# First two token groups of an FNet and ReGLU layer: one written order on all engines, GpSimd's subtractions behind VectorE's

## The chip, the cores and the metric

One core of a Trainium2 chip runs the whole program. The metric is the device time of one execution in microseconds (us), from the median of several runs; lower is better. The kernel before took 1047.72 us (median of three runs: 1047.72, 1048.57 and 1043.9).

## The reference

For 2048 tokens x of width 640, with xn = layernorm(x) over the width:

```python
a = einsum("bsd,ed->bse", xn, dft_hid_re)
b = einsum("bsd,ed->bse", xn, dft_hid_im)
y = einsum("ts,bse->bte", dft_seq_re, a) - einsum("ts,bse->bte", dft_seq_im, b)
gate, up = xn @ W_gate, xn @ W_up
h = gate * (gate > 0) * up
return x + y + h @ W_down
```

All of it is float32. The four DFT matrices are ordinary inputs.

## The kernel before

Every product is made of three TensorE passes. An operand is split into a rounded high part and a low part (operand minus high part), and a product is high x high, then high weights x low moving data, then low weights x high moving data (`mm3`, lines 125 to 131; the passes are lines 129, 130, 131). TensorE is so the engine with the most work, and the other engines make the high and low parts. Usually ScalarE writes the high part (line 123) and VectorE subtracts it (line 124).

The first stage multiplies the layer norm of the tokens by the sequence DFT. Tokens come in eight groups (`NG`) of 128 x 2; j = 0, 1 counts the two rows of tokens that a partition holds (`SG`). A unit of work is `first_stream(c, name, g)`: one block of 128 x 1024 of the DFT (`raw`, split into `cb`) for column chunk c and group n, multiplied with the normalised tokens of that group (`xs_early` for groups 0 to 3, `xs_late` for 4 to 7). Each unit has four steps: load, prepare, run, finish. `drive(4, 2)` issues them with the loads four units ahead and the preparing two units ahead. For an engine the order of its instructions is fixed when the program is built: a scheduler orders them, except where `tc.keep_in_program_order` pins an instruction to the place in which it was written, and where `tc.issue_after` puts it behind another. SP's queue issues the loads in its own order, and each load waits there for its buffer; GpSimd's queue issues the stores and small copies.

The normalisation of a group: VectorE takes statistics (`ln_stats`, lines 203 and 204), ScalarE and VectorE make the mean's negative and the inverse root (`ln_root`, lines 210 to 217, mostly instructions on 128 x 1 or 128 x 2 elements), then the normalised high part is written by ScalarE and the low part by VectorE.

The start is special, since nothing is there yet to multiply:

- TensorE first runs 48 products on zeros (line 111).
- `first_group` (lines 283 to 320) normalises group 0 one j at a time, columns d0 (128) before d14 (256), and splits the two DFT blocks c = 0 and c = 1 of group 0 in halves of 512 columns: ScalarE the high part (line 290), GpSimd the low part (line 291). VectorE writes the tokens' low parts in line 230. A dummy on GpSimd (line 299) makes it wait for line 217 before its first subtraction.
- `first_products(j, b)` (lines 474 to 484) runs 18 products for each j. A pass is v = 0 (high x high), 1 (low tokens) or 2 (low DFT). They may be interleaved by the scheduler.
- `second_group` (lines 263 to 282) normalises group 1 whole (both j at once): ScalarE writes the high parts (line 275), VectorE the scaled tokens (278) and the low parts (280). The DFT block of that group for c = 0 is split by the ordinary `split` (lines 123 and 124), placed by the scheduler.
- `second_products(b)` (lines 446 to 455) multiplies it: for j = 0 the passes v = 0 and 2, the same for j = 1, then v = 1 for both.
- From group 2 on `layernorm(g)` (lines 236 to 261) and `product` do the same with fewer rules.

A group's tokens lie in one of four places of a shared buffer (`ln_place`), so the load of group g + 4 waits until group g's last reader is done; for group 0 that is line 258, for ScalarE.

## Time and profile before

| | |
|---|---|
| median of three runs | 1047.72 us (1043.9 to 1048.57) |
| profiled execution, first to last instruction (span) | 1043.3 us |
| lowest of the three runs, beside that span | 1043.9 us, 0.6 us above it |
| TensorE busy | 1028.4 us of the span |
| first product of the first stage | starts at 6.62 us |
| first product of the second group | starts at 18.45 us |
| mean granted TensorE clock | 0.997 |

The profile has one execution. Its own run time is not listed apart from the three; the span is the nearest to the lowest run. A row of the timeline reads: start, duration, engine, line, operation, output and inputs, shape, count, and in brackets the idle time before it with what ended it. PE is TensorE's matmul, PEld its weight load, DVE VectorE, ACT ScalarE, POOL GpSimd, SPq the queue of SyncE. Rows of consecutive instructions of a kind are merged (x2, x32), and instructions of one engine overlap by some 0.1 us in such rows. The granted clock (PEclk) is the share of full speed that the throttle let through.

### The profile page before, as it was taken

The numbers are of one execution on the slowest core, as the hardware profiler recorded it, in microseconds if no ns is written. First come the engines' busy times: TensorE is split into PE (matmuls) and PEld (weight loads), VectorE is DVE, ScalarE is ACT, GpSimd is POOL, SyncE is SP. The second block draws the span as 40 slices with busy tenths as digits, with TensorE's granted clock in tenths as the row PEclk, the third lists the DMA queues.
The fourth block names the chain that finished last, engine by engine and source line by source line (L and its number), as shares of the span: only waits on it lengthen the run. The fifth ranks groups of instructions, "written<-read, shape, count | busy, mean of one in ns | idle before, by whom it ended". The sixth has DMA issues, their size and how long they took to land.

```text
span 1043.3 us, 12416 instructions
## 1 busy us (share of the span) xinstructions
PE 1028.4 (99%) x4528; PEld 847.3 (81%) x4528; DVE 802.1 (77%) x1071; ACT 433.5 (42%) x543; POOL 95.7 (9%) x156
## 2 busy tenths in 40 slices
PE   8999999999999899899999999999999999999998
PEld 7888888888887788688888888888888888888886
DVE  7857886978979887577887988887488667786764
ACT  6654453333333443333334534343355423552521
POOL 2000010101211001421110000100000000000000
PEclk9999999999999999999999999999999999999999
DMA  7985754958867863863364566565498637986454
GB/s 294 340 247 170 261 161 140 311 205 269 305 199 259 339 203 116 251 222 143 131 206 177 203 224 232 215 237 188 145 393 287 207 111 218 366 300 233 157 159 121
DMA packets 100156, 233.29 MB, mean 224 GB/s; under 512 B 11392, under 2 KB 50816, under 8 KB 98688
## 3 DMA queue, kind: packets, MB, share of 16 engines
q1 hardware_dynamic: 83664, 166.96, 47.6%
q0 software_dynamic: 16432, 65.55, 17.4%
q8 instruction: 35, 0.57, 0.2%
q14 instruction: 25, 0.20, 0.1%
HBM read 177.41 MB, written 54.02 MB: 222 GB/s over the span
## 4 chain that ended last, share of the span: by engine, by line
PE 84%; DMA 5%; DVE 5%; issue 4%; ACT 2%; POOL 0%; SPq 0%; ACTq 0%; POOLq 0%; DVEq 0%
PE ps L131 27%; PE ps L130 27%; PE ps L129 27%; DMA z<-in_wgu 2%; DVE cb L124 1%; DMA r<-in_x 1%; DMA st<-set 1%; PE ps L1147 1%; PE ps L483 1%; ACT cb L123 1%; DMA set<-st 1%; DMA rw<-hd 1%; DVE raw L595 0%; DVE gw L770 0%; ACT gw L120 0%
## 5 line engine op out<-in xcount | busy, mean ns | idle before, releaser
L131 PE MATMUL ps<-cb,wt 128*128 128x512 f32 x390 | 151.9, 390 | 0.1
L129 PE MATMUL ps<-cb,wt 128*128 128x512 f32 x390 | 151.8, 389 | 0.0
L130 PE MATMUL ps<-cb,wt 128*128 128x512 f32 x390 | 151.7, 389 | 0.0
L124 DVE TENSOR_TENSOR cb<-rw,cb 128x1024 fp32r<-128x1024 f32 x83 | 94.2, 1135 | 66.6 <-ACT cb L123 65.9
L123 ACT ACTIVATE cb<-rw 128x1024 fp32r<-128x1024 f32 x83 | 81.9, 987 | 145.2 <-PE ps L131 125.0
L123 ACT ACTIVATE cb<-raw 128x1024 fp32r<-128x1024 f32 x78 | 82.5, 1059 | 124.9 <-PE ps L131 108.3
L124 DVE TENSOR_TENSOR cb<-raw,cb 128x1024 fp32r<-128x1024 f32 x78 | 95.1, 1221 | 41.2 <-ACT cb L123 38.0
L130 PE MATMUL ps<-xs_early,gw 128*128 128x512 f32 x260 | 101.2, 389 | 0.0
L129 PE MATMUL ps<-xs_early,gw 128*128 128x512 f32 x260 | 101.2, 389 | 0.0
L131 PE MATMUL ps<-xs_early,gw 128*128 128x512 f32 x260 | 101.1, 389 | 0.0
L130 PE MATMUL ps<-cb,xs_late 128*128 128x512 f32 x256 | 99.8, 390 | 0.9 <-DVE cb L124 0.8
L131 PE MATMUL ps<-cb,xs_late 128*128 128x512 f32 x256 | 99.7, 389 | 0.3 <-DVE xs_late L251 0.3
L129 PE MATMUL ps<-cb,xs_late 128*128 128x512 f32 x256 | 99.6, 390 | 0.4 <-ACT cb L123 0.4
L130 PE MATMUL ps<-cb,xs_early 128*128 128x512 f32 x238 | 92.8, 390 | 1.5 <-DVE cb L124 1.5
L129 PE MATMUL ps<-cb,xs_early 128*128 128x512 f32 x238 | 92.6, 391 | 1.1 <-ACT cb L123 1.1
L120 ACT ACTIVATE gw<-z 128x1024 fp32r<-128x1024 f32 (+1 forms) x52 | 57.8, 1111 | 84.2 <-DVE z L760 68.7
L131 PE MATMUL ps<-cb,xs_early 128*128 128x512 f32 x238 | 92.1, 389 | 0.0
L131 PEld LDWEIGHTS ps<-cb,wt 128*128 128x128 f32 x390 | 73.2, 188 | 15.7 <-DVE wt L124 0.5
L130 PEld LDWEIGHTS ps<-cb,wt 128*128 128x128 f32 x390 | 73.2, 188 | 15.4
L129 PEld LDWEIGHTS ps<-cb,wt 128*128 128x128 f32 x390 | 73.2, 188 | 15.2
L120 ACT ACTIVATE u<-ps 128x512 f32<-128x512 f32 x52 | 31.2, 599 | 93.0 <-PE ps L131 93.0
L770 DVE TENSOR_TENSOR gw<-z,gw 128x1024 fp32r<-128x1024 f32 (+1 forms) x52 | 64.8, 1286 | 2.3 <-ACT gw L120 2.2
(192 smaller groups left out, 1932.1 us busy)
## 6 DMA issues: line engine op xcount, KB each, us to landing
raw<-in_dft SPq DMA_DIRECT2D x94, 512.0 KB, 5.7
wt<-wparts SPq DMA_DIRECT2D x66, 256.0 KB, 3.2
z<-in_wgu SPq DMA_DIRECT2D x26, 640.0 KB, 4.0
hd<-ob POOLq DMA_DIRECT2D x26, 512.0 KB, 3.5
rw<-hd SPq DMA_DIRECT2D x24, 512.0 KB, 6.1
wparts<-pw POOLq DMA_DIRECT2D x11, 1024.0 KB, 4.1
tk<-in_dft SPq DMA_DIRECT2D x16, 512.0 KB, 6.2
rw<-pq SPq DMA_DIRECT2D x16, 512.0 KB, 7.7
```

What stands on the lines that cost most here:

```text
L120: return nc.scalar.activation(o, i, AF.Copy)
L123: nc.scalar.activation(hi, src, AF.Copy)
L124: return nc.vector.tensor_tensor(lo, src, hi.bitcast(F32), op=OP.subtract)
L129: nc.tensor.matmul(ps, wh, mh, start=first, stop=False, skip_group_check=more)
L130: nc.tensor.matmul(ps, wh, ml, start=False, stop=False, skip_group_check=more)
L131: nc.tensor.matmul(ps, wl, mh, start=False, stop=last, skip_group_check=more)
L483: nc.tensor.matmul(E[c, key], xn_part(j, d)[v == 1], b[c][0][:, int(v == 2), j], start=j == 0 and v == 0, stop=False)
L770: tt(self.w[:, 1, cs], self.z[:, cs], self.w[:, 0, cs].bitcast(F32), op=OP.subtract)
L1147: nc.tensor.matmul(B[key], wr[:, v, es], hr[:, cs], start=False, stop=v == 1, skip_group_check=not new)
```

## The change

Only the start of the first stage is rewritten.

- Loads: the order becomes tokens j = 0, DFT (c = 0, j = 0), tokens j = 1, DFT (1, 0), (0, 1), (1, 1).
- `first_group` is one loop over j. For j = 1 the normalised high parts come from ScalarE in one step out of the raw tokens (new line 315, with the bias made in line 313), VectorE centres all 640 columns behind them (line 222) and then writes the low parts (317).
- GpSimd's two subtractions of a j (new line 295) stand behind a dummy (new `behind_vector`, line 268) that reads the last column of the tokens' low parts of that j: it waits until VectorE has written them.
- `first_products` takes the passes in the order v = 0 and 1 for c = 0, v = 0 and 1 for c = 1, then v = 2 for both, and all are pinned.
- `second_group` also splits the DFT block of group 1: its high part on ScalarE (line 277) ahead of `ln_root`, its low part on VectorE (line 285) as the last instruction of the group. Everything in it is pinned.
- `second_products` are pinned (line 462), and the products of n = 1, c = 1 stand behind their last one.

The numbers of instructions stay as they were but for a second dummy on GpSimd, two more rows on VectorE and one less on ScalarE. From about 60 us on, the order of every engine's instructions is the same as before.

```diff
--- before.py
+++ after.py
@@ -260,62 +260,69 @@
         if g == NG - 1:
             nc.sync.dma_start(rows.rearrange("m (g p j) -> p m g j", p=P, j=SG), stat)
 
-    def second_group():
+    def pin(steps):
+        return [tc.keep_in_program_order(i) for i in steps]
+
+    def behind_vector(src, o):
+
+        pin([nc.gpsimd.tensor_tensor(o, src, src, op=OP.mult)])
+
+    def second_group(b, raw):
 
         xs, bs, mv = ln_tiles(1)
         js = slice(0, SG)
         nm, r = (stat[:, i, 1, js] for i in range(2))
-        with tc.issue_after(late["ln"]):
-            for i in ln_stats(1, xs, bs, mv, js):
-                pass
-            for i in ln_root(1, mv, js):
-                tc.keep_in_program_order(i)
-            nmr = mv[:, js, 6]
-            late["ln"] = tc.keep_in_program_order(nc.vector.tensor_tensor(nmr, nm, r, op=OP.mult)).ins
-            highs = [nc.scalar.activation(xn_block(1, K14, 0)[:, j], xs[:, j, K14], AF.Identity,
-                                          bias=mv[:, j, 6:7], scale=stat[:, 1, 1, j : j + 1]) for j in range(SG)]
-            for j in range(SG):
-                nc.vector.tensor_scalar(xs[:, j], xs[:, j], mv[:, j, 0:1], stat[:, 1, 1, j : j + 1],
-                                        op0=OP.subtract, op1=OP.mult)
-            low = nc.vector.tensor_tensor(xn_block(1, K14, 1), xs[:, :, K14], xn_block(1, K14, 0).bitcast(F32), op=OP.subtract)
-            keep_a21(1)
-        late["first"] = [i.ins for i in highs + [low]]
+        nmr = mv[:, js, 6]
+        pin(ln_stats(1, xs, bs, mv, js))
+        pin([nc.scalar.activation(flat(b, 0), raw, AF.Copy)])
+        pin(ln_root(1, mv, js))
+        pin([nc.vector.tensor_tensor(nmr, nm, r, op=OP.mult)])
+        pin(nc.scalar.activation(xn_block(1, K14, 0)[:, j], xs[:, j, K14], AF.Identity,
+                                 bias=mv[:, j, 6:7], scale=stat[:, 1, 1, j : j + 1]) for j in range(SG))
+        pin(nc.vector.tensor_scalar(xs[:, j], xs[:, j], mv[:, j, 0:1], stat[:, 1, 1, j : j + 1],
+                                    op0=OP.subtract, op1=OP.mult) for j in range(SG))
+        pin([nc.vector.tensor_tensor(xn_block(1, K14, 1), xs[:, :, K14], xn_block(1, K14, 0).bitcast(F32), op=OP.subtract)])
+        late["ln"] = pin([nc.vector.tensor_tensor(flat(b, 1), raw, flat(b, 0).bitcast(F32), op=OP.subtract)])[0].ins
+        late["second"] = late["ln"]
+        keep_a21(1)
 
     def first_group(b):
 
 
-        pin = lambda steps: [tc.keep_in_program_order(i) for i in steps]
         xs, bs, mv = ln_tiles(0)
         part = lambda c, j: b[c][1][:, j * CH : (j + 1) * CH]
-        high = lambda c, j: [nc.scalar.activation(b[c][0][:, 0, j], part(c, j), AF.Copy)]
-        low = lambda c, j: [nc.gpsimd.tensor_tensor(b[c][0][:, 1, j], part(c, j), b[c][0][:, 0, j].bitcast(F32),
-                                                    op=OP.subtract)]
-        j0, j1 = slice(0, 1), slice(1, 2)
+        high = lambda c, j: pin([nc.scalar.activation(b[c][0][:, 0, j], part(c, j), AF.Copy)])
+        low = lambda c, j: pin([nc.gpsimd.tensor_tensor(b[c][0][:, 1, j], part(c, j), b[c][0][:, 0, j].bitcast(F32),
+                                                        op=OP.subtract)])
         d0, d14, rest, every = slice(0, P), slice(P, 3 * P), slice(P, D), slice(0, D)
-        pin(ln_stats(0, xs, bs, mv, j0))
-        pin(ln_center(0, xs, mv, 0, d0, nc.vector))
-        pin(ln_root(0, mv, j0))
-
-        pin([nc.gpsimd.tensor_tensor(mv[:, 0, 6:7], stat[:, 1, 0, 0:1], stat[:, 1, 0, 0:1], op=OP.mult)])
-        pin(high(0, 0))
-        pin(low(0, 0))
-        h0, h14 = ln_scale(0, xs, 0, d0), ln_scale(0, xs, 0, d14)
-        pin([next(h0)])
-        pin(ln_center(0, xs, mv, 0, rest, nc.vector))
-        pin([next(h14)])
-        pin(high(1, 0))
-        pin(low(1, 0))
-        pin(h0)
-        pin(h14)
-        pin(high(0, 1))
-        pin(low(0, 1))
-        pin(ln_stats(0, xs, bs, mv, j1))
-        pin(ln_root(0, mv, j1))
-        pin(ln_center(0, xs, mv, 1, every, nc.scalar))
-        pin(ln_scale(0, xs, 1, d0))
-        pin(ln_scale(0, xs, 1, d14))
-        pin(high(1, 1))
-        late["ln"] = pin(low(1, 1))[-1].ins
+        for j in range(SG):
+            js = slice(j, j + 1)
+            places = [tokens(0)[:, j * XS + o : j * XS + o + D] for o in (0, D)]
+            pin(ln_stats(0, xs, bs, mv, js))
+            if j == 0:
+                pin(ln_center(0, xs, mv, 0, d0, nc.vector))
+            pin(ln_root(0, mv, js))
+            high(0, j)
+            nmr = mv[:, j, 6:7]
+            if j == 0:
+                h0, h14 = ln_scale(0, xs, j, d0), ln_scale(0, xs, j, d14)
+                pin([next(h0)])
+                pin(ln_center(0, xs, mv, 0, rest, nc.vector))
+                pin([next(h14)])
+            else:
+                pin([nc.vector.tensor_tensor(nmr, stat[:, 0, 0, js], stat[:, 1, 0, js], op=OP.mult)])
+                for cs in (d0, d14):
+                    pin([nc.scalar.activation(places[0][:, cs], xs[:, j, cs], AF.Identity, bias=nmr, scale=stat[:, 1, 0, js])])
+                pin(ln_center(0, xs, mv, j, every, nc.vector))
+                h0, h14 = (pin([nc.vector.scalar_tensor_tensor(places[1][:, cs], xs[:, j, cs], stat[:, 1, 0, js],
+                                                               places[0][:, cs].bitcast(F32), op0=OP.mult, op1=OP.subtract)])
+                           for cs in (d0, d14))
+            high(1, j)
+            pin(h0 if j == 0 else ())
+            pin(h14 if j == 0 else ())
+            behind_vector(places[1][:, 3 * P - 1 : 3 * P].bitcast(F32), mv[:, j, 6:7] if j == 0 else bs[:, 0, 0, 0:1])
+            low(0, j)
+            low(1, j)
 
     def token_sets(q, step, stage=stage, unit=None):
 
@@ -452,7 +459,8 @@
             for j in js:
                 for v in vs:
                     for d, key in zip((0, 1, 4), keys):
-                        nc.tensor.matmul(E[0, key], xn_part(SG + j, d)[v == 1], b[:, int(v == 2), j], start=False, stop=False)
+                        start["pe"] = pin([nc.tensor.matmul(E[0, key], xn_part(SG + j, d)[v == 1], b[:, int(v == 2), j],
+                                                            start=False, stop=False)])[0].ins
 
     def product(g, b, w, accs, first, more, extra=None):
 
@@ -474,14 +482,13 @@
     def first_products(j, b):
 
         keys = [("e1", 0), ("e1", 1), "v1"]
-        for v, cs in (((0, (0,)), (1, (0,)), (2, (0,)), (0, (1,)), (1, (1,)), (2, (1,))),
-                      ((0, (0,)), (2, (0,)), (0, (1,)), (1, (0,)), (2, (1,)), (1, (1,))))[j]:
+        for v, cs in ((0, (0,)), (1, (0,)), (0, (1,)), (1, (1,)), (2, (0, 1))):
             for c in cs:
                 for d, key in zip((0, 1, 4), keys):
                     if j == 0 and v == 0:
                         E[c, key] = bank()
-                    nc.tensor.matmul(E[c, key], xn_part(j, d)[v == 1], b[c][0][:, int(v == 2), j],
-                                     start=j == 0 and v == 0, stop=False)
+                    pin([nc.tensor.matmul(E[c, key], xn_part(j, d)[v == 1], b[c][0][:, int(v == 2), j],
+                                          start=j == 0 and v == 0, stop=False)])
 
     def resident(g, d):
         return lambda j, i: xn_part(g * SG + j, d + i)
@@ -514,31 +521,36 @@
         def load():
             if n == 0 and c == 0:
                 st = start["raw"] = [raw(), raw()]
-                for j in range(SG):
-                    ln_load(0, slice(j, j + 1))
-                    for k in range(2):
-                        i = (k + j) % 2
-                        nc.sync.dma_start(st[i][:, j * CH : (j + 1) * CH], dft[i, 0, 0][:, j * CH : (j + 1) * CH])
+                get = lambda c, j: nc.sync.dma_start(st[c][:, j * CH : (j + 1) * CH], dft[c, 0, 0][:, j * CH : (j + 1) * CH])
+                ln_load(0, slice(0, 1))
+                get(0, 0)
+                ln_load(0, slice(1, 2))
+                for i in ((1, 0), (0, 1), (1, 1)):
+                    get(*i)
                 return
             if norm is not None:
                 tc.keep_in_program_order(ln_load(norm, slice(0, SG)))
             if n > 0 or c > 1:
                 t["s"] = raw()
                 nc.sync.dma_start(t["s"], dft[c, 0, n])
+                start[c, n] = t
 
         def prepare():
             if norm == 0:
                 start["b"] = [(parts(), st) for st in start["raw"]]
                 first_group(start["b"])
                 return
-            if norm is not None:
-                (second_group if norm == 1 else lambda: layernorm(norm))()
-            if n > 0 or c > 1:
+            if norm == 1:
+                t1 = start[0, 1]
+                t1["b"] = parts()
+                second_group(t1["b"], t1["s"])
+            elif norm is not None:
+                layernorm(norm)
+            if (n > 0 or c > 1) and "b" not in t:
                 t["b"] = b = parts()
-
                 with ExitStack() as order:
-                    for i in late["first"] if (c, n) == (1, 1) else ():
-                        order.enter_context(tc.issue_after(i))
+                    if (c, n) == (1, 1):
+                        order.enter_context(tc.issue_after(late["second"]))
                     split(flat(b, 0), flat(b, 1), t["s"])
 
         def run():
@@ -549,7 +561,10 @@
                 second_products(t["b"])
                 return
             accs = [(c, ("e1", i)) for i in range(2)]
-            product(g, t["b"], resident(n, 0), accs, half == 0, half == 1, ((c, "v1"), half, half == 0))
+            with ExitStack() as order:
+                if n == 1 and c < 2:
+                    order.enter_context(tc.issue_after(start["pe"]))
+                product(g, t["b"], resident(n, 0), accs, half == 0, half == 1, ((c, "v1"), half, half == 0))
 
         def finish():
             if g == NH - 1:
```

## The prediction

> **What bounds the kernel.** The page first.
>
> ```profile
> span 1043.3 us, 12416 instructions
> ...
> PE 1028.4 (99%) x4528; PEld 847.3 (81%) x4528; DVE 802.1 (77%) x1071; ACT 433.5 (42%) x543; POOL 95.7 (9%) x156
> ```
>
> TensorE is busy for all but 14.9 us of the span, so a change of the start is worth only what it takes from or adds to TensorE's waits there. Next, TensorE in the timeline of the start, and the windows:
>
> ```profile
> 6.62 0.50 PE L483 MATMUL ps<-cb,xs_early 128*128 128x512 f32 x1 [0.30 <-ACT xs_early L229]
> 8.02 0.98 PE L483 MATMUL ps<-cb,xs_early 128*128 128x512 f32 x3 [0.89 <-DVE xs_early L230]
> 9.44 9.17 PE L483 MATMUL ps<-cb,xs_early 128*128 128x512 f32 x32 [0.44 <-DVE xs_early L230]
> 18.45 2.88 PE L455 MATMUL ps<-cb,xs_early 128*128 128x512 f32 x12
> ...
> 22.52 0.39 PE L455 MATMUL ps<-cb,xs_early 128*128 128x512 f32 x1
> 22.75 0.39 PE L130 MATMUL ps<-cb,xs_early 128*128 128x512 f32 x1
> ...
> 43.84 0.50 PE L131 MATMUL ps<-cb,xs_late 128*128 128x512 f32 x1 [0.30 <-DVE xs_late L251]
> ...
> 6.57:9.98 3.41, 2.02 (x6) 1.00 0.99 385
> 9.98:13.40 3.42, 3.42 (x9) 0.50 1.02 420
> ```
>
> Products at full clock start 0.227 us apart (22.52 to 22.75). The 36 first products need 8.2 us and take 11.8 (6.62 to 18.45). The 3.6 us over are two waits for VectorE's low tokens (line 230) and a stretch of 3.42 us at half clock (the 0.50 in the second window row; its columns are length, busy time, clock, DMA share, GB/s), in which 9 products lie where 15 would start. From 18.45 on TensorE doesn't wait, until a wait for group 4's low tokens at 43.84. All that the start could give is these 3.6 us and some 0.5 at 43.84.
>
> **The change, part by part.**
>
> ```profile
> 5.98 0.16 DVE L217 SCALAR_TENSOR_TENSOR stat<-mv 128x1 f32<-128x1 f32 x1
> 6.17 0.91 ACT L229 ACTIVATE xs_early<-r,stat 128x128 fp32r<-128x128 f32 x2
> 6.22 0.36 POOL L299 TENSOR_TENSOR mv<-stat 128x1 f32<-128x1 f32 x1 [5.77 <-DVE stat L217]
> 6.55 2.55 POOL L291 TENSOR_TENSOR cb<-raw,cb 128x512 fp32r<-128x512 f32 x2
> 6.61 2.77 DVE L230 SCALAR_TENSOR_TENSOR xs_early<-r,stat,xs_early 128x128 fp32r<-128x128 f32 x2
> 9.30 0.87 DVE L203 BATCH_NORM_STATS2 bs<-r 128x6 f32<-128x320 f32 x2
> 9.79 1.28 POOL L291 TENSOR_TENSOR cb<-raw,cb 128x512 fp32r<-128x512 f32 x1 [0.69 <-ACT cb L290]
> 10.21 0.21 DVE L204 BATCH_NORM_AGGREGATE mv<-bs 128x2 f32<-128x12 f32 x1
> 11.06 0.16 DVE L215 SCALAR_TENSOR_TENSOR mv<-mv 128x1 f32<-128x1 f32 x1
> 11.26 0.16 DVE L216 TENSOR_TENSOR mv<-mv 128x1 f32<-128x1 f32 x1
> 11.45 0.16 DVE L217 SCALAR_TENSOR_TENSOR stat<-mv 128x1 f32<-128x1 f32 x1
> 11.92 0.80 ACT L229 ACTIVATE xs_early<-r,stat 128x128 fp32r<-128x128 f32 x2
> 12.36 0.35 DVE L230 SCALAR_TENSOR_TENSOR xs_early<-r,stat,xs_early 128x128 fp32r<-128x128 f32 x1 [0.35 <-ACT xs_early L229]
> 13.03 0.47 DVE L230 SCALAR_TENSOR_TENSOR xs_early<-r,stat,xs_early 128x256 fp32r<-128x256 f32 x1
> 13.42 0.20 DVE L204 BATCH_NORM_AGGREGATE mv<-bs 128x2 f32<-128x12 f32 x1
> 14.41 0.21 DVE L204 BATCH_NORM_AGGREGATE mv<-bs 128x2 f32<-128x12 f32 x1
> 14.54 1.22 DVE L124 TENSOR_TENSOR cb<-raw,cb 128x1024 fp32r<-128x1024 f32 x1
> 16.60 0.17 DVE L274 TENSOR_TENSOR mv<-stat 128x2 f32<-128x2 f32 x1
> 16.80 1.31 ACT L275 ACTIVATE xs_early<-r,mv,stat 128x384 fp32r<-128x384 f32 x2 [1.57 <-DVE mv L274]
> 19.38 0.94 DVE L280 TENSOR_TENSOR xs_early<-r,xs_early 128x768 fp32r<-128x768 f32 x1
> 20.36 1.17 DVE L124 TENSOR_TENSOR cb<-raw,cb 128x1024 fp32r<-128x1024 f32 x1
> 23.77 0.61 DVE L246 TENSOR_SCALAR r<-r,mv,stat 128x640 f32<-128x640 f32 x1
> ```
>
> 1. *Low tokens of j = 0.* The pair of line 230 takes 0.35 and 0.47 alone (12.36, 13.03), but 2.77 beside GpSimd's two subtractions (2.55): each waits until one has ended. Behind the dummy they are alone: the second starts when ScalarE's high part is there (6.17 + 0.91 = 7.08, so 7.11) and ends at 7.58 instead of 9.38, 1.80 us sooner.
>
> 2. *GpSimd* starts its dummy 0.08 behind VectorE, as before (6.22 after 5.98 + 0.16) at 7.67, the subtractions 0.33 after it at 7.99, and they end at 9.26 and 10.54, where they ended at 7.8 and 9.1. The new pass order asks for them last: 12 products come first, 6.62 to 9.7. The first is in time, the second about 0.1 late.
>
> 3. *Statistics and root of j = 1* took 2.31 (9.30 to 11.45 + 0.16) and now start at 7.50. They fall beside the subtractions. In the trace nothing shows an instruction of one element with two inputs beside a running subtraction: line 215 starts at 11.06, at which the third (9.79 + 1.28) ends. So bounds: nothing, as the one-input lines 203 and 204 kept their time there (0.87 for two, 0.21), or a wait to the end of the second subtraction. Line 216 would be due at 7.50 + (11.26 - 9.30) = 9.46 and wait to 10.54, 1.08 us; if line 215 at 9.26 waits already, 1.28. The nearest row is line 230, the same operation with two inputs, which waited out each subtraction: I take 1.1. The root ends at 7.50 + 2.31 + 1.1 = 10.9.
>
> 4. *The rest of j = 1.* The bias (new line 313) is one step more, some 0.25 behind line 217 (an estimate: the root's own steps are 0.20 apart, 11.26 to 11.45, and this one waits for ScalarE too), and ScalarE follows 0.20 behind it (16.60 to 16.80): 11.2. Two high parts 0.80: 12.0. Then VectorE, which waits for them, centres 640 columns (0.61, as line 246) and writes the low parts (0.82 less 0.1 of overlap): 13.4, where they ended at 13.50. The early start is spent; without the wait of step 3 it is 12.3. GpSimd's second pair then runs from 13.84 to 16.4.
>
> 5. *First products.* Without the waits of 1.4 and 0.8 us the window from 6.57 has 14 starts instead of 6, so the half clock after it goes. They run into j = 1's parts instead: high tokens at 11.6 and 12.05, low ones at 13.0 and 13.4, GpSimd's at 15.1 and 16.4. The last three start from 16.45, and all end at about 17.1 instead of 18.45.
>
> 6. *Second group: what is late next.* VectorE's order is now four statistics, root, bias, scaling, low tokens, and **last** the low part of the DFT block (new line 285). In the trace that subtraction ran at 14.54, before the root, and was done at 15.76, and TensorE came at 18.45. Now: statistics from 13.3; the first aggregate 0.91 later (9.30 to 10.21), the second 0.99 after it, as 13.42 to 14.41, so at 15.2. Line 215 follows 0.85 later (10.21 to 11.06) at 16.05, which again meets GpSimd's last subtraction (to 16.4, 0.3 us); line 217 at 16.8, the bias at 17.05, the high parts from 17.25 to 18.56. Each scaling waits for ScalarE's high part of its j, and the second ends at 19.2. Then 0.94 for the low tokens and 1.2 for line 285 give **21.25** (without the waits of steps 3 and 6: 19.95).
>
> The passes of j = 0 are v = 0, then v = 2, which reads line 285's output. TensorE does three products when the first high part comes (17.96) and stands from 18.7 to 21.3. The other 15 and the product behind them need 15 x 0.227 + 0.1 = 3.5, so line 130 starts at 24.8 instead of 22.75: **2.05 us later**. Behind line 285 on VectorE stand group 2's statistics and the low part of the next block. The trace began that subtraction at 20.36; now it follows four statistics and an aggregate (1.7 by lines 203 and 204) and begins at 22.85, 2.5 us later and just in time for TensorE.
>
> 7. *What is carried to 43.84.* TensorE's 2.05 could use up the 0.46 us that it waited there, but group 4's low tokens come by VectorE, whose delay is 2.5.
>
> ```profile
> 25.66 0.89 ACT L258 ACTIVATE st<-r,stat 128x256 f32<-128x256 f32 x2
> 26.58 0.33 SPq L198 DMA_DIRECT2D r<-in_x  x1
> ...
> r<-in_x SPq DMA_DIRECT2D x1, 640.0 KB, 4.3
> ...
> 33.90 1.28 DVE L203 BATCH_NORM_STATS2 bs<-r 128x6 f32<-128x320 f32 x3 [0.94 <-DMA r<-in_x]
> 42.29 1.49 DVE L251 TENSOR_TENSOR xs_late<-r,xs_late 128x1280 fp32r<-128x1280 f32 x1
> ```
>
> Group 4's tokens are loaded by SP at 26.58, when line 258 has ended, and land 7.3 us later, at 33.9, after a wait of 0.94 on VectorE. The load of group 5's, issued just ahead of it (the row of 640 KB), took 4.3. In the new order of SP one DFT load stands ahead of it, and line 258 is some 2.85 us later (2.5 and a longer root), so the issue is at 29.4. After 4.3 us it would be there at 33.7, after 7.3 at 36.7. Group 4's statistics now also stand ahead of group 3's low tokens (0.95 us). From landing to the end at 43.78 the trace took 9.9; now it is 10.8. So the delay at 43.84 lies between 0.7 and 3.7; I take the middle, 2.2, near to TensorE's own 2.05. Later orders are unchanged.
>
> The moved loads cost nothing: they are as many bytes, and the tokens of j = 1, now third, land before 7.50.
>
> **Sum: +2.2 us**, 1043.3 to 1045.5 on the span. The lowest run, 1043.9, is 0.6 above that span, the median 1047.72 is 4.4 above it; on the median the forecast is **1049.9**. A measurement can tell about 0.5% (5.2 us) from no change, so this is "same".
>
> [...]
>
> **The rivals.**
>
> *No lock for one element.* Line 285 ends at 19.95, line 130 starts at 23.5, 0.7 late; with VectorE's 1.3 us of delay the end is +1.0: 1048.7. For: lines 203 and 204 weren't held. Against: line 230 was.
>
> *A new half clock.* If the window from 16.81 again has few products (5 or 6 starts by step 6; 6 starts before), the next runs at half. From 21.3 to 23.64 TensorE starts 5.5 products instead of 10.3, 1.1 us: +3.1, 1050.8. For: 2.02 of 3.41 us busy was followed by 0.50. Against: where the windows lie need not repeat from run to run. [...]
>
> *The gain stays (faster).* If the second group's parts were there when TensorE gets to them, the first products end at 16.15 (step 3 without wait) and 2.3 us are kept: 1045.4. For: all waits at 8.02 and 9.44 go. Against: it decides by line 285 being done before 17, and the order puts it behind two scalings that need ScalarE.
>
> *Slower by more than 0.5%.* Group 4's tokens. If their load lands 7.3 us after its issue, at 36.7, group 3's low tokens behind them are late for TensorE and group 4's end at 47.5: +3.7; with a half clock behind that stand (1.7, half of 3.42) +5.4: 1053.1. It decides from a landing at about 35. For: the 7.3 and the load now ahead of it. Against: the load of group 5 took 4.3.
>
> **How the numbers follow.** Forecast 0.40, no lock 0.22, half clock 0.20, slower 0.10, gain stays 0.08. The range reaches from the kept gain to just over the half clock with the upper end of step 7: 1045.0 to 1052.5; it leaves out the slowest. Over 0.5% faster 0.04 (half of the last rival, as the runs spread over 4.7 us), slower 0.10, within 0.86.
>
> **What would show it.** Line 230's pair in 1.0 us: step 1. Line 215 or 216 with a hole in front that ends with a subtraction: step 3; no hole: the first rival. TensorE idle before the fourth of line 462 with VectorE's line 285 as releaser: step 6. Line 130 behind line 462 at 24.8; the clock from 20.2 on; the wait before group 4's statistics: the others. The forecast is wrong if line 285 ends before 18, or if the delay is used up by later waits of TensorE.

## The result and the profile after

The kernel after takes 1051.2 us (median of 20 executions, 1046.31 to 1054.21), the kernel before 1047.16 (20 executions, 1043.9 to 1051.28): ratio 1.0036, 95% interval 1.0022 to 1.0049. So it is some 4 us slower, within the 0.5% that the forecast called "same". It stood at 1049.9, with a range of 1045.0 to 1052.5. The profiled execution of after took 1047.28 us with a span of 1045.4. That is **2.1 us** over the span of before, where the forecast had 2.2, but only half of what the medians differ by. In every run that lists both, the time is 1.7 to 2.1 us over the span. So the profiled execution of before took about 1045.1 us (an estimate from its span of 1043.3), some 2 us below its median, while that of after lies 3.9 us below its own: the two profiles are not of typical executions, and that of before isn't of the lowest run, 1043.9. Where the other half is, is the question of the experiments.

The page of after, its first lines:

```profile
span 1045.4 us, 12416 instructions
...
PE 1028.8 (98%) x4528; PEld 846.1 (81%) x4528; DVE 802.0 (77%) x1073; ACT 433.2 (41%) x542; POOL 95.5 (9%) x157
```

TensorE works as long as before (1028.8 us against 1028.4); what was added is waiting. Its timeline at the start, of after (start, length, instruction, in brackets the idle time ahead of it and what ended that):

```profile
6.65 4.77 PE L490 MATMUL ps<-cb,xs_early 128*128 128x512 f32 x18 [0.48 <-ACT xs_early L229]
11.65 1.23 PE L490 MATMUL ps<-cb,xs_early 128*128 128x512 f32 x3 [0.23 <-ACT xs_early L315]
13.12 4.14 PE L490 MATMUL ps<-cb,xs_early 128*128 128x512 f32 x15 [0.24 <-DVE xs_early L317]
17.76 0.97 PE L462 MATMUL ps<-cb,xs_early 128*128 128x512 f32 x3 [0.50 <-ACT xs_early L280]
21.14 3.74 PE L462 MATMUL ps<-cb,xs_early 128*128 128x512 f32 x15 [2.40 <-DVE cb L285]
```

The first products end at 17.26 instead of 18.61 (9.44 + 9.17 in the profile of before; its next product started at 18.45), without the old waits and without half clock. Then three products of the second group run, and TensorE stands 2.40 us for line 285, the low part of the DFT block. VectorE and GpSimd in the same view of after, where this comes from:

```profile
6.63 0.35 DVE L230 SCALAR_TENSOR_TENSOR xs_early<-r,stat,xs_early 128x128 fp32r<-128x128 f32 x1
7.13 0.48 DVE L230 SCALAR_TENSOR_TENSOR xs_early<-r,stat,xs_early 128x256 fp32r<-128x256 f32 x1 [0.15 <-ACT xs_early L229]
7.70 0.19 POOL L268 TENSOR_TENSOR mv<-xs_early 128x1 f32<-128x1 f32 x1 [7.25 <-DVE xs_early L230]
7.86 2.54 POOL L295 TENSOR_TENSOR cb<-raw,cb 128x512 fp32r<-128x512 f32 x2
9.30 1.12 DVE L215 SCALAR_TENSOR_TENSOR mv<-mv 128x1 f32<-128x1 f32 x1
10.45 0.16 DVE L216 TENSOR_TENSOR mv<-mv 128x1 f32<-128x1 f32 x1
...
12.71 0.75 DVE L317 SCALAR_TENSOR_TENSOR xs_early<-r,stat,xs_early 128x128 fp32r<-128x128 f32 x2
...
16.80 0.16 DVE L279 TENSOR_TENSOR mv<-stat 128x2 f32<-128x2 f32 x1
17.74 1.21 DVE L282 TENSOR_SCALAR r<-r,mv,stat 128x640 f32<-128x640 f32 x2 [0.78 <-ACT xs_early L280]
18.99 0.96 DVE L284 TENSOR_TENSOR xs_early<-r,xs_early 128x768 fp32r<-128x768 f32 x1
19.86 1.22 DVE L285 TENSOR_TENSOR cb<-raw,cb 128x1024 fp32r<-128x1024 f32 x1
```

Read it from the top: the low tokens are alone and short (0.35, 0.48). GpSimd then runs from 7.86 to 10.40, and line 215, one element with two inputs, takes 1.12 us instead of 0.16 and ends at 10.42, just behind GpSimd. Everything on VectorE up to line 285, the last of its written order, is late by that and by the order itself, and 285 ends at 21.08.

**A table by place.** All kernels run the same 4480 products (products of zeros not counted), so one can ask when the n-th starts. Worked out from the trace records: the delay in us of each kernel against the profiled execution of before, whose own starts head the columns (the 36th is the last of the first products, the 54th lies at the end of the second group's). The last column is each kernel's ratio, less 1, times 1047 us, with its 95% interval; it differs by up to 0.7 us from the difference of the two medians. (The other kernels are those of the experiments below.)

| kernel | 36th (18.22) | 54th (22.30) | 1300th (305.85) | 1790th (422.40) | 1850th (441.43) | last | by ratio |
|---|---|---|---|---|---|---|---|
| after | -1.4 | +2.2 | +1.7 | +0.6 | +1.8 | +2.1 | +3.8 (2.3 to 5.1) |
| after, again | -1.4 | +2.1 | +1.7 | +0.1 | +2.0 | +2.7 | +4.1 (2.4 to 5.7) |
| before, again | -1.8 | -0.9 | -1.3 | -2.5 | +0.4 | +0.2 | -1.2 (-2.8 to 0.5) |
| low part first | -1.4 | -0.6 | +1.9 | +2.0 | +3.9 | +4.9 | +4.4 (2.6 to 6.2) |
| low DFT passes last | -1.4 | +0.3 | +2.8 | +2.0 | +4.0 | +3.9 | +3.2 (1.5 to 4.9) |
| second subtraction later | -1.9 | +3.0 | +2.4 | +4.6 | +6.8 | +7.0 | +2.6 (1.3 to 4.0) |
| wait filled | -1.5 | +2.1 | +1.6 | +0.3 | +1.0 | +1.0 | +1.0 (-0.3 to 2.4) |
| first part only | -0.1 | +0.7 | +1.9 | +1.6 | +3.7 | +4.7 | +2.9 (1.6 to 4.3) |
| second part only | -1.6 | +3.3 | +2.7 | +2.2 | +5.3 | +5.4 | +4.1 (2.5 to 5.7) |
| second part only, filled | -0.3 | +2.0 | +1.4 | +0.8 | +1.4 | +2.2 | 0.0 (-1.6 to 1.6) |
| orders mended | -1.8 | -1.2 | -0.9 | -0.3 | +2.9 | +3.6 | +1.8 (0.3 to 3.4) |
| mended and filled | -1.8 | -1.2 | -1.0 | +0.2 | +3.0 | +4.8 | +0.7 (-0.6 to 2.1) |
| before, filled | -1.7 | -0.8 | -1.1 | -2.2 | -0.6 | +0.7 | -1.4 (-2.7 to 0.0) |

From 80 to 328 us the delays stay as they are; from there to 445 us they change by up to 4.4 us, though the instructions of that stretch stand in the same order in before and after. In the rows of the trace they change in two places: from 328 to 357 us, where TensorE waits for DFT splits, and from 425 to 441 us, where it waits for the gate weights.

### The profile page after: what moved, and what is told of

Its sections match the earlier page's. It is cut to its first block, busy times and chain, and to the rows that moved or that the text cites. A ratio compares the mean times of both kernels' runs of the same rounds, so it can differ in the third digit from the quotient of the medians.

```text
span 1045.4 us, 12416 instructions
## 1 busy us (share of the span) xinstructions
PE 1028.8 (98%) x4528; PEld 846.1 (81%) x4528; DVE 802.0 (77%) x1073; ACT 433.2 (41%) x542; POOL 95.5 (9%) x157
## 4 chain that ended last, share of the span: by engine, by line
PE 87%; DVE 6%; DMA 4%; ACT 1%; issue 1%; SPq 0%; DVEq 0%; ACTq 0%
PE ps L131 29%; PE ps L130 29%; PE ps L129 28%; DMA z<-in_wgu 2%; DVE cb L124 2%; DMA tk<-in_dft 1%; PE ps L1162 1%; DVE raw L610 1%; DMA wr<-in_wd 1%; DVE tk L610 0%; ACT cb L123 0%; DVE gw L785 0%; PE ps L462 0%; DVE sa L500 0%; ACT gw L120 0%
```

## The experiments

**Theory A**: the wait for line 285 costs its length, and half clock behind it costs more in the executions where it falls so. **The rivals**: the first part (line 215's 1.12 us beside GpSimd's subtraction, step 3) is the loss; or the loss comes from 330 us on. Each expectation says what its own theory A and B (or rival) are for that run.

### Low part of the DFT block before the scaling

```diff
         pin(nc.scalar.activation(xn_block(1, K14, 0)[:, j], ...) for j in range(SG))
+        pin([nc.vector.tensor_tensor(flat(b, 1), raw, ...)])
         pin(nc.vector.tensor_scalar(xs[:, j], ...) for j in range(SG))
-        pin([nc.vector.tensor_tensor(xn_block(1, K14, 1), ...)])
-        late["ln"] = pin([nc.vector.tensor_tensor(flat(b, 1), raw, ...)])[0].ins
+        low = pin([nc.vector.tensor_tensor(xn_block(1, K14, 1), ...)])[0]
+        late["ln"] = low.ins
```

> The changed kernel with one instruction of VectorE moved: the low part of group 1's DFT block (line 285) stands between the bias and the scaling (the time in which VectorE waits for ScalarE, 16.96 to 17.74 us in the changed kernel's trace). Theory A (what the change loses is TensorE's wait of 2.4 us for that low part, and a half clock behind it in some runs): no wait at the fourth product of the second group, its 18 products in one stretch from about 17.8 to 22.0, the product behind them at 22.0 instead of 24.5, and 2 to 4 us less than the changed kernel: 1047 to 1049, about the kernel before or up to 1 us less. Rival B (the loss comes with group 4's tokens, later loads or VectorE's order from 24 us on, and TensorE would lose it there anyway): the wait goes, but another of about 2 us comes before 60 us, and the time stays at 1050 to 1052.

Measured: 1051.25 us (6 executions), ratio 1.0042 (1.0025 to 1.0059). TensorE's timeline of this kernel:

```profile
17.75 4.38 PE L463 MATMUL ps<-cb,xs_early 128*128 128x512 f32 x18 [0.53 <-ACT xs_early L280]
...
28.93 0.50 PE L129 MATMUL ps<-cb,xs_early 128*128 128x512 f32 x1 [2.27 <-ACT xs_early L120]
```

The wait is gone and another of 2.27 us stands 8 us later. It ends with group 2's high tokens. VectorE had put two more DFT splits into group 2's root (line 124 at 22.93 and 24.10, then line 215 at 25.22), and ScalarE a third ahead of the high part itself (line 123 at 27.11, line 120 at 28.05). Taking away one wait moved it: 0.6 us ahead at the 54th product, 1.9 late at 306 us, near after's 1.7. Theory A's number fell with it; the time and the new wait are those of rival B. What was wrong was to treat line 285 as the only thing late.

### The passes that read the low DFT part last

```diff
-        for js, vs in (((0,), (0, 2)), ((1,), (0, 2)), ((0, 1), (1,))):
+        for js, vs in (((0,), (0,)), ((1,), (0,)), ((0, 1), (1,)), ((0, 1), (2,))):
```

> The changed kernel with another order of passes in the second products: v = 0 for both j, then the low tokens (v = 1), then the low part of the DFT block (v = 2) last. VectorE's order stays. Theory A: two short waits instead of the one of 2.4 us (about 0.7 us for the low tokens, which end at 19.95, next to none for the low part of the block at 21.1), the product behind at 22.8 to 23.0 instead of 24.5; 1.5 to 3 us less than the changed kernel, 1048 to 1050, like the kernel before. Rival B: as before, 1050 to 1052.

Measured: 1049.85 us (9 executions), ratio 1.0031 (1.0014 to 1.0047). The wait of 2.40 shrinks to 0.58 and the next product starts at 22.79, as theory A had it, but group 2's high tokens stop TensorE again, as TensorE's timeline of this kernel shows:

```profile
19.93 3.02 PE L462 MATMUL ps<-cb,xs_early 128*128 128x512 f32 x12 [0.58 <-DVE xs_early L284]
...
29.82 0.49 PE L129 MATMUL ps<-cb,xs_early 128*128 128x512 f32 x1 [2.24 <-ACT xs_early L120]
```

The time lies just inside theory A's range, 0.15 us from rival B's: it is 1.4 us below after by the medians, which the intervals don't separate.

### GpSimd's second subtraction behind the next root

```diff
                 pin([nc.vector.tensor_tensor(nmr, stat[:, 0, 0, js], ...)])
+                behind_vector(nmr, mv[:, 0, 6:7])
+                low(1, 0)
...
             low(0, j)
-            low(1, j)
+            if j == 1:
+                low(1, j)
```

> The changed kernel with GpSimd's second subtraction of j = 0 (block c = 1) behind a dummy that waits for the bias of j = 1 (line 313), so that no subtraction runs beside the root of j = 1. Theory A with the lock: line 215 of j = 1 takes 0.16 instead of 1.12 us, the root ends about 1.0 sooner, the low part of group 1's block about 0.7 to 1.0 sooner (20.1 to 20.4), TensorE's wait stays at about 2.4 and ends that much sooner; 0.5 to 1 us less than the changed kernel. The low part of block c = 1, j = 0 comes about 1 us later, which TensorE waits for once, at about 11. Rival (line 215 is long for another reason, such as its wait for ScalarE): it stays at 1.1 us and nothing is gained.

Measured: 1049.82 us (12 executions), ratio 1.0025 (1.0012 to 1.0038). GpSimd and VectorE in this kernel's timeline:

```profile
7.78 1.28 POOL L295 TENSOR_TENSOR cb<-raw,cb 128x512 fp32r<-128x512 f32 x1
9.21 0.16 DVE L215 SCALAR_TENSOR_TENSOR mv<-mv 128x1 f32<-128x1 f32 x1
9.87 0.16 DVE L313 TENSOR_TENSOR mv<-stat 128x1 f32<-128x1 f32 x1
10.31 1.27 POOL L295 TENSOR_TENSOR cb<-raw,cb 128x512 fp32r<-128x512 f32 x1
```

With nothing of GpSimd beside it line 215 takes 0.16 us again and line 313 starts 1.04 us earlier than in after (9.87, 10.91): step 3 is shown from both sides. Line 285 ends 0.74 us sooner than in after (20.34), as expected, and the time is 1.4 us below after's, which the intervals don't separate. But TensorE now waits 1.11 us for that subtraction, and still 2.42 for line 285. And behind that wait stands what one rival had foretold, in TensorE's windows of this kernel (length, busy time, products that lie in it, granted clock, DMA share, GB/s):

```profile
17.73:21.14 3.41, 0.99 (x5) 1.00 0.78 309
21.14:24.55 3.41, 3.41 (x9) 0.50 0.85 282
24.55:27.97 3.42, 3.42 (x16) 1.00 0.55 224
```

In the window behind the wait TensorE runs at half clock. The same windows of after, where the wait lies over the border of two windows:

```profile
16.10:19.51 3.41, 2.13 (x7) 1.00 1.00 399
19.51:22.93 3.42, 1.79 (x8) 1.00 0.55 162
22.93:26.34 3.41, 3.41 (x17) 1.00 0.97 389
```

Nothing was slowed here. So the profiled execution of after is one of those that got the wait without its half clock.

### The wait filled

38 products of zeros, into a bank of their own, between the third and the fourth product of line 462. They add nothing to the result and wait for nothing.

```diff
+        fill = bank()
...
                         start["pe"] = pin([nc.tensor.matmul(E[0, key], ...)])[0].ins
+                    if j == 0 and v == 0:
+                        pin(nc.tensor.matmul(fill[:, :P], warm, warm, start=True, stop=True) for _ in range(38))
```

> The changed kernel with 38 products on zeros (128 x 128, bf16, about 2.1 us at full clock) put on TensorE between the third and the fourth product of the second group, in a PSUM bank that nothing reads: they lie in the wait for line 285 and keep TensorE busy there. They add nothing to the result. Theory A with a half clock: the profiled run of the changed kernel had no half clock at the start, but its 20 runs have a median 4 us above the kernel before where its trace shows 2.1; if the rest is a half clock that follows the wait in most runs, the filled kernel keeps the wait and loses the half clock: 1 to 2 us less than the changed kernel's median, 1049 to 1050. Rival: the rest of the difference comes from later places, and the time stays at 1051 (or rises by up to 0.3 us if the zeros reach beyond the wait).

Measured: 1047.97 us (12 executions), ratio 1.0010 (0.9997 to 1.0023). TensorE's timeline of this kernel:

```profile
18.49 2.29 PE L467 MATMUL ps<-warm 128*128 128x128 bf16 x38
21.06 3.69 PE L464 MATMUL ps<-cb,xs_early 128*128 128x512 f32 x15 [0.28 <-DVE cb L286]
```

The fourth product starts at 21.06 (21.14 in after): the wait is as long as it was, and at 306 us the delay is 1.6 (1.7 in after). The 38 products take 2.29 us, where 2.1 was the author's estimate. Only TensorE's idleness is gone, and 3.2 us of the median with it, more than theory A had asked for (the intervals of the two kernels, in the table, just touch).

### One half of the change at a time

First part only: loads, `first_group` and `first_products` of after, `second_group` and `second_products` of before. Second part only: the other way round. Neither needs a line that isn't in one of the two kernels.

> The first part of the kernel after (the low tokens of the first slice alone, GpSimd's dummy, the new order of the first products) with the second group and the second products of the kernel before. Theory A (the loss is the wait for the low part of the DFT block, and the half clock that it can draw): the first products end near 17.1 us instead of 18.45, the low part of the DFT block is not in the way, so there is no wait over 1 us before 24 us and the kernel is as fast as before or up to 1.5 us faster: 1045.5 to 1047.5. Theory B (the loss comes from the first part, because GpSimd's lock delays VectorE by 1.1 us and with it the second group's tokens): TensorE waits for the second group's tokens, and the time is 1048.5 to 1051.

> The first part of the kernel before with the second group and the second products of the kernel after, in their written order. Theory A: the first products end at 18.45 us as before, the low part of the DFT block is still last in VectorE's written order, so TensorE waits for it until about 21 to 22 us, 1.5 to 2 us; the time is 1048.5 to 1051. Theory B: no lock, no delay, no loss: 1046.5 to 1048.

Measured: first part only 1049.88 us (12 executions), ratio 1.0028 (1.0015 to 1.0041); second part only 1051.23 (9 executions), 1.0039 (1.0024 to 1.0054). The first part falls into theory B's numbers, the second just above theory A's: each half loses, so neither theory holds alone. TensorE of the first part alone:

```profile
13.41 3.19 PE L491 MATMUL ps<-cb,xs_early 128*128 128x512 f32 x12 [0.51 <-DVE xs_early L319]
17.53 0.96 PE L491 MATMUL ps<-cb,xs_early 128*128 128x512 f32 x3 [0.93 <-POOL cb L297]
18.95 3.00 PE L464 MATMUL ps<-cb,xs_early 128*128 128x512 f32 x12 [0.46 <-ACT xs_early L282]
28.40 0.50 PE L129 MATMUL ps<-cb,xs_early 128*128 128x512 f32 x1 [0.98 <-ACT xs_early L120]
```

Behind the first product there is no wait of a microsecond, but four of 0.5 to 1 us, the last again for group 2's high tokens. With the scheduler's order for the second group, the low part of its DFT block (line 124, 1.81 us instead of 1.22) meets GpSimd's late second pair, which takes 3.50 us instead of 2.54, as this kernel's timeline shows:

```profile
13.97 3.50 POOL L297 TENSOR_TENSOR cb<-raw,cb 128x512 fp32r<-128x512 f32 x2
14.54 1.81 DVE L124 TENSOR_TENSOR cb<-raw,cb 128x1024 fp32r<-128x1024 f32 x1
17.11 0.38 DVE L215 SCALAR_TENSOR_TENSOR mv<-mv 128x2 f32<-128x2 f32 x1
```

Line 215 of the second group is long here too: it takes 0.38 us and ends at 17.49, just behind GpSimd (17.47).

The second part alone has after's wait behind before's first part, and in its profiled execution the half clock behind it. Its windows on TensorE:

```profile
6.80:10.21 3.41, 2.12 (x7) 1.00 0.98 378
10.21:13.62 3.41, 3.41 (x16) 1.00 1.02 418
17.04:20.45 3.41, 0.97 (x4) 1.00 0.83 338
20.45:23.86 3.41, 2.89 (x7) 0.50 0.70 230
```

At 306 us it is 2.7 late, after 1.7: the half clock is worth about 1.0 there (1.3 against the same kernel with its wait filled, 1.4 late in the table). The first two rows say something else. This kernel has before's early waits, and no half clock followed them. The stretch at half clock that step 5 had booked as a gain (9.98 to 13.40 of before) is missing here.

### The kernel before again, and its early waits filled

Unchanged; and with 13 and 6 products of zeros in the waits of 0.89 and 0.44 us, the first six products pinned in the order that they had.

> The kernel before, unchanged, as a second profile of it and as a measure of what the comparison gives for no change. Theory A (the profiled execution of before had a short wait and a single stretch at half clock near 433 to 440 us, which its typical executions don't): 1046.5 to 1048, ratio within 0.9985 to 1.0015, and the second profile shows a wait over 4 us there or two stretches, about 1 to 2 us more than the first one between 403 and 443 us. Theory B (before really passes that place faster than every other kernel): the same wait of 3.7 us and one stretch again.

> The kernel before with its two early waits of TensorE (0.89 and 0.44 us) filled with 13 and 6 products of zeros into a bank of their own; the first six products in the order that they had. Theory A (the half clock of 9.98 to 13.40 us follows the early waits, and cost the first products 1.35 to 1.7 us): no half clock before 20 us, first products end near 17 us, but the second group's tokens set the start of the next ones, so that 0 to 1.4 us come out: 1045.5 to 1047.2. Theory B (that stretch comes from the time before the first product, or costs nothing): 1046.5 to 1048, with the stretch or without.

Measured: before again 1046.25 us (12 executions), ratio 0.9989 (0.9973 to 1.0005), which is what the comparison gives for no change; before filled 1046.16 (12 executions), 0.9987 (0.9974 to 1.0000). The filled one lies in theory A's range, with no half clock at the start of its profile. But the unfilled one took 1046.25, so that filling these early waits gained anything isn't shown. The second profile of before, TensorE's timeline:

```profile
9.31 7.55 PE L483 MATMUL ps<-cb,xs_early 128*128 128x512 f32 x32 [0.46 <-DVE xs_early L230]
17.42 3.02 PE L455 MATMUL ps<-cb,xs_early 128*128 128x512 f32 x12 [0.57 <-ACT xs_early L275]
```

The 32 products took 7.55 us here and 9.17 in the first profile: in this execution too there was no half clock at the start. It is 1.3 us ahead at 306 us, and against it after is 3.0 late there, not 1.7. Yet it ends level with the first (+0.2). The reason stands in the timeline of this second profile around 430 us:

```profile
426.43 0.33 SPq L750 DMA_DIRECT2D z<-in_wgu  x1
430.36 0.39 PE L131 MATMUL ps<-xs_early,gw 128*128 128x512 f32 x1
435.31 1.06 ACT L120 ACTIVATE gw<-z 128x1024 fp32r<-128x1024 f32 x1 [9.37 <-DMA z<-in_wgu]
436.90 0.79 PE L129 MATMUL ps<-r,gw 128*128 128x512 f32 x1 [6.16 <-ACT p L120]
```

and in that of the first profile of before:

```profile
428.83 0.33 SPq L750 DMA_DIRECT2D z<-in_wgu  x1
435.29 1.06 ACT L120 ACTIVATE gw<-z 128x1024 fp32r<-128x1024 f32 x1 [6.88 <-DMA z<-in_wgu]
436.88 0.79 PE L129 MATMUL ps<-r,gw 128*128 128x512 f32 x1 [3.67 <-ACT p L120]
```

TensorE came 2.5 us earlier, the load of the gate weights was issued 2.4 us earlier, and took 8.9 us to its first reader instead of 6.5. The next product started at 436.90 and 436.88. In after the same load took 6.8 (429.57 to 436.33) and TensorE went on at 437.93. In before again theory A's signs are there: its second profile has a wait over 4 us and two windows at half clock (434.12 to 440.95), though the time lies 0.25 us below theory A's range. So here this place swallowed a lead, and the spread of that load from one execution to the next, 2 us and more, is as large as what is to be measured.

### The orders mended

The low part first, GpSimd's second subtraction later, and the DFT splits of the third group's blocks behind that group's scaling (VectorE) and high part (ScalarE); then the same with 17 products of zeros in the wait that is left. The first two edits are those above, and the third, shortened, is:

```diff
+                    if n == 2 and c < 2:
+                        with tc.issue_after(late[2][1] if c else late["second"]):
+                            nc.scalar.activation(flat(b, 0), t["s"], AF.Copy)
+                        with tc.issue_after(late[2][0]):
+                            nc.vector.tensor_tensor(flat(b, 1), t["s"], ...)
+                    else:
+                        split(flat(b, 0), flat(b, 1), t["s"])
-                    split(flat(b, 0), flat(b, 1), t["s"])
```

> The kernel after with three orders changed: the low part of the second DFT block before the scaling (as in the run with the low part first), GpSimd's second subtraction of the first slice behind the next slice's root (as in the run with the later subtraction), and the DFT splits of the third group's two blocks behind the third group's scaling on VectorE and its high part on ScalarE, which removes what held group 2's high tokens until 28.9 us. Theory A (waits in the first 30 us are the loss, each worth its length): no wait over 1 us before 30 us, TensorE at or ahead of the kernel before at 26 us, 1045 to 1046.8. Theory B (the delay is made up or made again later, at the gate weights' landing near 433 us): 1047 to 1050 though the early waits are gone.

> The kernel with the three orders mended, and the 1.06 us that TensorE still waits for GpSimd's second subtraction filled with 17 products of zeros into a bank of their own. Theory A (a wait costs its length and, in some executions, half clock behind it): no wait over 0.6 us in the first 30 us, TensorE at the same places as in the kernel with the mended orders, time 1046.5 to 1048.5, at most 1.5 below it. Theory B (what that kernel loses, it loses from 330 us on): 1048 to 1050, no gain.

Measured: 1048.93 us (12 executions), ratio 1.0017 (1.0003 to 1.0032), and filled 1048.75 (12 executions), 1.0007 (0.9994 to 1.0020). TensorE's timeline of the unfilled one:

```profile
6.68 4.01 PE L495 MATMUL ps<-cb,xs_early 128*128 128x512 f32 x15 [0.35 <-ACT xs_early L229]
11.75 5.05 PE L495 MATMUL ps<-cb,xs_early 128*128 128x512 f32 x21 [1.06 <-POOL cb L297]
17.13 4.39 PE L467 MATMUL ps<-cb,xs_early 128*128 128x512 f32 x18 [0.32 <-ACT xs_early L281]
```

Behind the last of these lines there is no wait of 0.6 us until 334 us. This is what the change would have needed: 0.9 us ahead of the first profile of before at 306 us, though 0.4 behind the second. It brings nothing at the end: both profiles lose about 3 us from 422 to 441 us. Theory B has it here, and neither version beats before.

### After again, and the second part filled

> The kernel after, unchanged, for a second profile of it beside the others. Theory A (between the 2.1 us of the trace and the 4.0 us of the medians lie half-clock stretches that most executions have and the profiled one had not): 1050 to 1051.5, and if the profiled execution is a typical one of 0.995 it shows two or more stretches at half clock besides the one near 436 us, each worth up to 1.7 us where TensorE does not wait. Theory B (the rest lies in the landing of the gate weights, whose wait near 433 us differs between executions): the same time, one stretch at half clock, and a wait over 5 us there.

> The first part of the kernel before with the second group and second products of the kernel after (1051.2 us without the filling), and TensorE's wait of 2.42 us for the low part of the DFT block filled with 38 products of zeros, as it was filled in the kernel after. The wait stays, only TensorE's idleness goes. Theory A (behind that wait the half clock follows in many executions, and it is worth 1 us where it does): 1049.8 to 1051. Theory B (filling it is worth about 3 us, as the medians of the filled kernel after say): 1047.5 to 1049. In both, the profiled execution has no half clock between 17 and 28 us, and TensorE's delay against the kernel before at 306 us is near 1.7 us instead of 2.7.

Measured: after again 1051.41 us (12 executions), ratio 1.0039 (1.0023 to 1.0054); its profile has a span of 1046.0 and one stretch at half clock behind a wait of 4.5 us near 434 us, so it shows neither theory's cause of the slower executions. Its time agrees with both. The second part filled takes 1047.37 (12 executions), 1.0000 (0.9985 to 1.0015), **3.9 us** below the same kernel with an idle wait. TensorE's timeline of the filled one:

```profile
18.87 2.29 PE L461 MATMUL ps<-warm 128*128 128x128 bf16 x38
20.98 3.67 PE L458 MATMUL ps<-cb,xs_early 128*128 128x512 f32 x15
```

The fourth product of the second group starts at 20.98 with the filling and at 20.97 without. The time lies 0.1 us below theory B's range, and so on its side, a second time: filling is worth more than the 1 us that the half clock costs up to 306 us.

## Why the prediction held, step by step

- **Step 1** (low tokens alone): right. They ended at 7.61, forecast 7.58.
- **Step 2** (GpSimd): right. The pair ran from 7.86 to 10.40, forecast 7.99 to 10.54.
- **Step 3** (line 215's wait beside GpSimd's subtraction): right, and the point where it decided. Line 215 took 1.12 us, and 0.16 with the subtraction moved. The rival "no lock for one element" is refuted: line 215, one element with two inputs, ended 0.02 us behind GpSimd's pair (10.42, 10.40), as the larger line 230 of before ended behind its subtractions (2.77 us for the pair beside them, 0.35 and 0.47 alone). The second wait of this kind (0.3 us in step 6) could not show: line 215 started at 16.14 and took 0.16, so that its own end lay behind GpSimd's (16.23) anyway.
- **Step 4**: right. Low tokens of j = 1 ended at 13.46, forecast 13.4.
- **Step 5** (first products end at 17.1): right for the place, 17.26, but the gain was booked against one execution. Of four profiles with before's early waits, two have half clock in the first products (before, and the second part filled, at 8.97), two have none (before again, second part alone). Against the second profile of before the 36th product of after starts 0.4 us later (-1.4 and -1.8 in the table), not 1.4 earlier.
- **Step 6**: right to 0.2 us. Line 285 ended at 21.08 (21.25), the next block's subtraction on VectorE began at 22.66 (22.85), and the 54th product is 2.2 us late (2.05).
- **Step 7** (group 4's tokens, +2.2): within its bounds, at the early end. The load was issued at 28.94 (29.4) and group 4's statistics began at 33.66 (33.7 to 36.7). After's timeline has no wait near 44 us, so what was carried on is TensorE's own delay less the 0.46 us that before lost there, 1.7 us instead of 2.2. The rival "slower" fell with it.
- **The sum**: 2.2 on the span, measured 2.1. The 1.7 of 306 us became 0.6 by 422 and 1.8 by 441; that it ends near 2.2 is in part the chance of that place.
- **"The gain stays"**: refuted, since line 285 came at 21, not before 17.
- **"A new half clock"**: it is shown, and the weight of 0.20 was too small. Of four profiles with an idle wait of 2.4 us, two have half clock behind it. The forecast added a span difference to a median as if the executions of both kernels differed by one number. The medians of after and of the second part alone lie 3.2 and 3.9 us above those with the wait filled, where the wait stayed as it was.

What is shown, then: the idle wait for line 285 costs the kernel most of its 4 us, and it costs them less by its length than by TensorE's idleness, since with the wait kept and filled what remains is +1.0 (-0.3 to 2.4) and 0.0 (-1.6 to 1.6). That half clock behind the wait is the way is argued, not shown in full. It is there in two profiles and worth 1.0 us up to 306 us; the other 2 to 3 us would have to arise from 330 us on, where the two profiles with it gain another 2.6 and 4.5 us of delay, but some without it as much (2.8 in the first part alone, 4.5 in the orders mended). The two profiles with it, and the orders mended, have a window at half clock from 337 to 360 us (355.65, 341.30 and 337.88), which no other profile has; but the orders mended and filled lose 5.8 us behind 306 us without one.

The granted clock that is listed for every execution says a little more. Its mean is 0.9946 in the 32 executions of after and 0.9963 with the wait filled, 0.9934 in the second part alone and 0.9950 filled. One window of 3.41 us at half clock is 0.0016 of the span, so filling took away about one such window per execution, worth up to 1.7 us (an estimate from these means). Yet about the same gain in clock (0.9947 to 0.9964 and 0.9947 to 0.9968) brought the orders mended 0.2 us and before 0.1 by the medians. So typical executions do have fewer such windows when the wait is filled, but that this is all that filling is worth isn't shown.

Two things stay open: why filling the wait for line 285 is worth so much, and why the first part alone, with few stretches at half clock (its mean clock is 0.9966), is 2.9 us slower.

## What to carry to other kernels

An engine's written order is only as good as its last line: ask which product needs each result first, and note that a mended wait shows the next one (here group 2's tokens, behind line 285). Compare a change of 0.3% with two profiles of the kernel before: one stretch at half clock that one execution had, and the next had not, was booked as a gain of 1.4 us. If a wait of TensorE can't be removed, filling it with products of zeros is worth a try: it took 3.2 and 3.9 us off for the wait of 2.4 us in two kernels, and some 0.2 us or less, by the medians, for the shorter waits in two others.

## What the runs showed of the hardware

- **The half clock came in whole windows of 3.41 us, whose place differed between executions.** In before it lasted from 9.98 to 13.40 us and again from 436.65 to 440.06, 125 windows later; in after from 435.94 to 442.77, two windows, and from 1043.52 to the end of the span; in before again from 434.12 to 440.95, two windows. In the 14 traces, counted by the products that lie in a window (a full one has 16 or 17): at full clock, each of the 28 windows with six or fewer was followed by half clock, of ten with seven products two were, and with eight or more none was but one that held seven products and five of zeros (second part filled, 5.56 us). Busy time doesn't order them: a window with 2.02 us busy and 6 products was followed by half clock (before, 6.57 us), and one with 1.79 us busy and 8 products was not (after, 19.51 us).
- **A load issued 2.4 us earlier did not land earlier.** The gate weights' second load took 6.5, 8.9 and 6.8 us to their first reader in three profiles with the same order of instructions, and that reader started at 435.29 and 435.31 in the two of before although the loads were issued 2.4 us apart.
